# Twenty short VectorE memsets and fifty-one one-element ScalarE copies at the start of a channel-attention kernel

## The chip, the cores and the metric

The kernel runs on one core of one Trainium2 chip. The metric is the device time of one execution in microseconds (us). Before the change it was 743.04 us, the median of 3 runs (742.54 to 744.04).

## The reference, cut to what matters

```python
H = W = 384; C = 384; r = C // 4          # x is (1, H, W, C) bf16, w1 (C, r), w2 (r, C)

def reference(x, w1, w2):
    xf = x.reshape(B, H * W, C)
    gap = jnp.mean(xf, 1)                 # mean over all pixels, per channel
    gmp = jnp.amax(xf, 1)                 # maximum over all pixels, per channel
    h_a = relu(gap @ w1)                  # (written as h * (h > 0))
    h_m = relu(gmp @ w1)
    scale = sigmoid(h_a @ w2 + h_m @ w2)
    return x * scale[:, None, None, :]
```

The scale needs all of `x` before any of the output can be written. So the kernel has a reading half (sums and maxima), a short turn in which the scale is made, and a storing half (multiply and store; what did not fit on chip is read again). On chip, `x` lies in six buffers, the slots.

## The kernel before

All engines share the tile `small`; the first lines fill its constants. ScalarE's only early work is a one-element Sigmoid.

```python
small = consts.tile([P, 16], BF16)
ones_bf = small[:, 0:1]
hid = small[0:R, 8:9]
hid_a = small[0:R, 10:12].bitcast(F32)
nc.vector.memset(ones_bf, 1.0)
pick = small[0:NQP, 10:10 + 2 * CQ].bitcast(F32)
nc.vector.memset(pick, 0.0)
for q in range(CQ):
    nc.vector.memset(pick[q * QP:q * QP + 1, q:q + 1], 1.0)
...
nc.scalar.activation(out=scale_bc[0:1, 0:1], in_=pick[0:1, 0:1], func=ACT.Sigmoid)
acc = consts.tile([P, A, C], BF16)
slots = [xpool.tile([P, n, C], BF16, name=f"x{s}") for s, n in enumerate(SLOTS)]
...
# reading half, one round per load: SyncE loads, TensorE sums, VectorE keeps the maximum
nc.sync.dma_start(out=rows[:, a:b, :], in_=...)
sums(rows, m, done, TOT - tail_rows)
nc.vector.tensor_tensor(out=acc[:, 0:k, :], in0=acc[:, 0:k, :], in1=rows[:, j:j + k, :], op=ALU.max)
...
# the turn, ScalarE's branch (mean) and VectorE's branch (maximum), which meet in hid
nc.scalar.activation(out=hid_a, in_=hTa_ps, func=ACT.Relu)
...   # acc folded to one row, transposed on TensorE, reduced, multiplied with w1
nc.vector.scalar_tensor_tensor(out=hid, in0=hTm_ps, scalar=0.0, in1=hid_a, op0=ALU.max, op1=ALU.add)
nc.tensor.matmul(z_ps, lhsT=hid.to_broadcast([R, P]), rhs=w2_sb, start=True, stop=True)
nc.scalar.activation(out=scale_bc, in_=z_ps, func=ACT.Sigmoid)
...
# storing half: VectorE multiplies, ScalarE issues the store, SyncE reads the next block into the slot
```

Of the kernel before, what the change touches and what calls it, by code (L numbers as in the profile page):

```python
# [32 lines left out]
ACC_STORES_AT = 3  # L33
SUM_TAIL = 2
MM_ROWS = 4


@with_exitstack
def kernel(
# [7 lines left out]
    nc = tc.nc  # L47
# [36 lines left out]
    small = consts.tile([P, 16], BF16)  # L84
# [8 lines left out]
    nc.vector.memset(pick, 0.0)  # L93
    for q in range(CQ):
        nc.vector.memset(pick[q * QP:q * QP + 1, q:q + 1], 1.0)
    ident_bf = consts.tile([P, P], BF16)
    make_identity(nc, ident_bf)

# [5 lines left out]
        scale_bc[0:NQP, 0:2 * P].bitcast(F32),  # L104
    ]
    nc.scalar.activation(out=scale_bc[0:1, 0:1], in_=pick[0:1, 0:1], func=ACT.Sigmoid)
    acc = consts.tile([P, A, C], BF16)
    slots = [xpool.tile([P, n, C], BF16, name=f"x{s}") for s, n in enumerate(SLOTS)]

# [3 lines left out]
    kept_ps = psum.tile([P, PSUM_ROWS, C], BF16)  # L113
    sum_ps = bank_a[0:NQP, 0:MM_ROWS * P]
    nc.vector.memset(bank_a, 0.0)
# [23 lines left out]
    def sums(rows, n, done, total):  # L139
        for k in range(0, n, MM_ROWS):  # L140
            g = min(MM_ROWS, n - k)
            for q in range(CQ):
                nc.tensor.matmul(  # L143
                    sum_ps[q * QP:q * QP + 1, 0:g * P],
                    lhsT=ones_bf[:, 0:1],
                    rhs=rows[:, k:k + g, q * P:(q + 1) * P],
                    start=(done + k == 0),
                    stop=(done + k + g == total),
                )

    def turn_sums():

        for r in range(MM_ROWS):
            nc.scalar.copy(out=s_sb[r % 2], in_=sum_ps[:, r * P:(r + 1) * P])
# [163 lines left out]
```

## Time and profile before

| | before |
|---|---|
| time, median of 3 | 743.04 us |
| bytes moved, mean rate | 312.32 MB, 421 GB/s |
| busy: VectorE (DVE), TensorE (PE), ScalarE (ACT) | 66%, 17%, 0% |
| DMA share in the turn, 268 to 277 us | 0.43 |

From the page of the kernel before: busy us of each engine with its share of the span and number of instructions; then the busy tenths of the 16 DMA engines and their GB/s in 40 equal slices; then the DMA queues with packets, MB and share of the engines' time.

```profile
PE 127.2 (17%) x966; PEld 40.6 (5%) x966; DVE 489.4 (66%) x168; ACT 3.3 (0%) x9; POOL 0.7 (0%) x6
DMA  9999999999999969999999999999999999999997
GB/s 383 423 435 434 433 430 418 428 429 426 427 422 422 418 254 378 402 435 446 432 431 428 432 437 436 436 432 432 427 434 437 436 436 432 432 427 432 441 437 340
q1 hardware_dynamic: 12032, 198.92, 63.2%
q8 instruction: 7, 0.11, 0.1%
q14 instruction: 4, 0.03, 0.0%
```

The DMA row is at nine tenths everywhere but in the turn and at the end: the kernel is bound by its transfers. ScalarE does next to nothing. The two "instruction" queues carry the engines' own instructions, 16 KB a packet on q8 and 8 KB on q14 (0.11 MB over 7, 0.03 MB over 4).

The timeline of the kernel before, VectorE and then ScalarE from the start. Columns: start, duration, engine, line, operation, output and input with their shapes, count, and in brackets how long the engine was idle and what ended that.

```profile
0.81 0.06 DVE L89 MEMSET small<- 128x1 bf16 x1 [0.81 <-PEq L302]
1.48 0.27 DVE L95 MEMSET small<- 1x1 f32 x3
7.18 1.26 DVE L179 COPY acc<-x_79 128x4224 bf16<-128x4224 bf16 x1 [5.44 <-DMA x_79<-in_x_dram]
0.73 1.28 ACT L106 ACT_TABLE_LOAD   x1 [0.73 <-PEq L302]
2.03 0.20 ACT L106 ACTIVATE scale_bc<-small 1x1 bf16<-1x1 f32 x1
266.97 0.26 ACT L154 COPY w_sb<-bank_a 65x128 f32<-65x128 f32 x1 [264.74 <-PE bank_a L143]
```

VectorE has nothing to do from 1.75 to 7.18 us, because the first tile is still on its way. ScalarE has nothing from 2.23 to 266.97 us. These two holes are where the change puts its instructions.

The view by windows of the kernel before: length, busy us (and instructions) of PE, PEld, DVE, ACT and POOL, granted clock, DMA share, GB/s.

```profile
268.00:277.00 9.00, 4.28 (x64) 3.47 (x63) 6.84 (x10) 1.27 (x5) 0.00 (x0) 0.50 0.43 115
```

And the end of the turn in the chain of work that ended last (start, duration, what):

```profile
275.61 0.17 DVE small L219
275.82 0.51 PE bank_a L220
276.41 0.50 ACT scale_bc L221
```

In the turn the DMA engines wait for the scale, so lateness there should go into the time in full.

### The profile page before, as it was taken

How to read it: one execution, taken by the hardware profiler on the slowest of the kernel's cores; microseconds unless marked ns; L12 is line 12 of the kernel's file. 1: busy time of each engine (PE TensorE's matmuls, PEld its weight loads, DVE VectorE, ACT ScalarE, POOL GpSimd, SP SyncE). 2: the span in 40 equal slices, each digit the busy share in tenths (PEclk: the TensorE clock that was granted, in tenths of full speed). 3: DMA queues.
4: the chain of work that ended last, by engine and by line, in shares of the span. 5: the costliest groups of instructions: out<-in, count | busy, mean ns of one | idle time of the engine just before them, and what ended most of it. 6: DMA issues, size and time to landing. Idle time of an engine off the chain costs nothing.

```text
span 741.5 us, 2477 instructions
## 1 busy us (share of the span) xinstructions
PE 127.2 (17%) x966; PEld 40.6 (5%) x966; DVE 489.4 (66%) x168; ACT 3.3 (0%) x9; POOL 0.7 (0%) x6
## 2 busy tenths in 40 slices
PE   3345443445454550000000000000000000000000
PEld 0011111111111120000000000000000000000000
DVE  6789999999999989999444443444444444444600
ACT  0000000000000000000000000000000000000000
POOL 0000000000000000000000000000000000000000
PEclk9865666655555555555555555555555555555555
DMA  9999999999999969999999999999999999999997
GB/s 383 423 435 434 433 430 418 428 429 426 427 422 422 418 254 378 402 435 446 432 431 428 432 437 436 436 432 432 427 434 437 436 436 432 432 427 432 441 437 340
DMA packets 18379, 312.32 MB, mean 421 GB/s; under 512 B 2400, under 2 KB 3008, under 8 KB 6592
## 3 DMA queue, kind: packets, MB, share of 16 engines
q1 hardware_dynamic: 12032, 198.92, 63.2%
q10 hardware_dynamic: 6336, 113.25, 35.7%
q8 instruction: 7, 0.11, 0.1%
q14 instruction: 4, 0.03, 0.0%
HBM read 198.92 MB, written 113.25 MB: 421 GB/s over the span
## 4 chain that ended last, share of the span: by engine, by line
another core or an unknown queue 44%; DMA 34%; DVE 14%; DVEq 1%; SPq 1%; issue 1%; PE 0%; ACT 0%; ACTq 0%
DMA x_81<-in_x_dram 9%; DMA x_82<-in_x_dram 7%; DVE acc L183 7%; DMA out_dram<-x_83 6%; DMA x_79<-in_x_dram 6%; DMA x_80<-in_x_dram 3%; DMA x_83<-in_x_dram 3%; DVE x_81 L226 1%; DVE x_80 L226 1%; DVE x_83 L226 1%; DVE x_82 L226 1%; DVE x_79 L226 1%; DVEq L313 1%; SPq L253 1%
## 5 line engine op out<-in xcount | busy, mean ns | idle before, releaser
L226 DVE TENSOR_TENSOR x_79<-x_79,scale_bc 128x16896 bf16<-128x16896 bf16 (+6 forms) x13 | 45.4, 3538 | 34.2 <-DMA x_79<-in_x_dram 33.0
L226 DVE TENSOR_TENSOR x_80<-x_80,scale_bc 128x16896 bf16<-128x16896 bf16 (+4 forms) x9 | 40.9, 4576 | 28.7 <-DMA x_80<-in_x_dram 28.7
L226 DVE TENSOR_TENSOR x_84<-x_84,scale_bc 128x16896 bf16<-128x16896 bf16 x4 | 35.8, 8958 | 33.1 <-DMA x_84<-in_x_dram 33.1
L226 DVE TENSOR_TENSOR x_83<-x_83,scale_bc 128x16896 bf16<-128x16896 bf16 x4 | 35.8, 8956 | 33.0 <-DMA x_83<-in_x_dram 33.0
L226 DVE TENSOR_TENSOR x_82<-x_82,scale_bc 128x16896 bf16<-128x16896 bf16 x4 | 35.8, 8957 | 32.8 <-DMA x_82<-in_x_dram 32.8
L226 DVE TENSOR_TENSOR x_81<-x_81,scale_bc 128x16896 bf16<-128x16896 bf16 (+3 forms) x6 | 36.0, 6021 | 31.0 <-DMA x_81<-in_x_dram 31.0
L183 DVE TENSOR_TENSOR acc<-acc,x_84 128x4224 bf16<-128x4224 bf16 (+3 forms) x21 | 47.3, 2253 | 5.4 <-DMA x_84<-in_x_dram 4.7
L143 PEld LDWEIGHTS <-small 128*1 128x1 bf16 x900 | 36.4, 110 | 229.9 <-issue 227.0
L183 DVE TENSOR_TENSOR acc<-acc,x_83 128x4224 bf16<-128x4224 bf16 (+1 forms) x19 | 42.8, 2253 | 1.3 <-DMA x_83<-in_x_dram 0.7
L183 DVE TENSOR_TENSOR acc<-acc,x_80 128x4224 bf16<-128x4224 bf16 (+1 forms) x18 | 40.6, 2257 | 3.0 <-DMA x_80<-in_x_dram 2.4
L183 DVE TENSOR_TENSOR acc<-acc,x_79 128x4224 bf16<-128x4224 bf16 (+1 forms) x17 | 38.9, 2287 | 1.5 <-DMA x_79<-in_x_dram 1.0
L183 DVE TENSOR_TENSOR acc<-acc,x_81 128x4224 bf16<-128x4224 bf16 (+2 forms) x17 | 37.9, 2229 | 1.5 <-DMA x_81<-in_x_dram 1.0
L183 DVE TENSOR_TENSOR acc<-acc,x_82 128x4224 bf16<-128x4224 bf16 x16 | 37.7, 2358 | 1.5 <-DMA x_82<-in_x_dram 1.0
L143 PE MATMUL bank_a<-x_84,small 128*1 128x512 bf16 (+2 forms) x165 | 21.6, 558 | 27.1 <-DMA x_84<-in_x_dram 27.1
L143 PE MATMUL bank_a<-x_79,small 128*1 128x512 bf16 (+1 forms) x150 | 20.4, 574 | 28.7 <-DMA x_79<-in_x_dram 28.7
L143 PE MATMUL bank_a<-x_80,small 128*1 128x512 bf16 (+3 forms) x150 | 21.0, 585 | 23.6 <-DMA x_80<-in_x_dram 23.6
L143 PE MATMUL bank_a<-x_83,small 128*1 128x512 bf16 (+2 forms) x159 | 20.3, 540 | 23.3 <-DMA x_83<-in_x_dram 23.3
L143 PE MATMUL bank_a<-x_82,small 128*1 128x512 bf16 (+2 forms) x138 | 19.6, 594 | 20.9 <-DMA x_82<-in_x_dram 20.9
L143 PE MATMUL bank_a<-x_81,small 128*1 128x512 bf16 (+3 forms) x138 | 19.4, 593 | 21.1 <-DMA x_81<-in_x_dram 21.1
L179 DVE COPY acc<-x_79 128x4224 bf16<-128x4224 bf16 x1 | 1.3, 1260 | 5.4 <-DMA x_79<-in_x_dram 5.4
L185 DVE COPY kept_ps<-x_79 128x3072 uint32<-128x3072 uint32 x1 | 3.4, 3354 | 0.0
L226 DVE TENSOR_TENSOR x_81<-kept_ps,scale_bc 128x6144 bf16<-128x6144 bf16 x1 | 3.4, 3350 | 0.0
(39 smaller groups left out, 22.5 us busy)
## 6 DMA issues: line engine op xcount, KB each, us to landing
x_84<-in_x_dram SPq DMA_DIRECT2D x5, 4224.0 KB, 27.4
x_79<-in_x_dram SPq DMA_DIRECT2D x5, 4224.0 KB, 27.4
x_80<-in_x_dram SPq DMA_DIRECT2D x5, 4224.0 KB, 27.7
x_81<-in_x_dram SPq DMA_DIRECT2D x5, 4224.0 KB, 27.4
x_82<-in_x_dram SPq DMA_DIRECT2D x5, 4224.0 KB, 27.4
x_83<-in_x_dram SPq DMA_DIRECT2D x4, 4224.0 KB, 27.4
out_dram<-x_82 ACTq DMA_DIRECT2D x4, 4224.0 KB, 74.3
out_dram<-x_83 ACTq DMA_DIRECT2D x4, 4224.0 KB, 71.1
```

The source lines that it names most:

```text
L143: nc.tensor.matmul(sum_ps[q * QP:q * QP + 1, 0:g * P], lhsT=ones_bf[:, 0:1], rhs=rows[:, k:k + g, q * P:(q + 1) * P], start=(done + k == 0 ...
L179: nc.vector.tensor_copy(out=acc, in_=rows[:, 0:A, :])
L183: nc.vector.tensor_tensor(out=acc[:, 0:k, :], in0=acc[:, 0:k, :], in1=rows[:, j:j + k, :], op=ALU.max)
L185: nc.vector.tensor_copy(out=kept_ps.bitcast(U32), in_=rows.bitcast(U32))
L226: nc.vector.tensor_tensor(out=dst, in0=src, in1=scale_bc.unsqueeze(1).to_broadcast([P, n, C]), op=ALU.mult)
L253: nc.sync.dma_start(out=slots[s][:, j:j + m, :], in_=rows_of(xr, first, n)[:, j:j + m, :])
L313: with _tile.TileContext(nc) as tc:
```

## The change

It adds 20 memsets of one element on VectorE and 51 copies of one element on ScalarE, near the start. They write columns of `small` that nothing reads. Their only possible use is to delay these two engines a little or to shift what comes later in their instruction streams.

```diff
+FILLS = (20, 51)
 ...
     for q in range(CQ):
         nc.vector.memset(pick[q * QP:q * QP + 1, q:q + 1], 1.0)
+    for _ in range(FILLS[0]):
+        nc.vector.memset(small[0:1, 9:10], 0.0)
 ...
     nc.scalar.activation(out=scale_bc[0:1, 0:1], in_=pick[0:1, 0:1], func=ACT.Sigmoid)
+    for _ in range(FILLS[1]):
+        nc.scalar.copy(out=small[0:1, 1:2], in_=small[0:1, 0:1])
```

## The prediction

> **What bounds the kernel now.** The page gives 312.32 MB moved in a span of 741.5 us at a mean of 421 GB/s; its DMA row shows 9 tenths in every slice but two. DVE is busy 66%, PE 17%, ACT 0% (3.3 us). The kernel is bound by DMA transfers; at the 432 GB/s that most slices show, 312.32 MB alone would take about 723 us (an estimate from the page). The other 18 us are the start (0 to 5 us: DMA share 0.67 in the view by windows), the turn between the reading half and the storing half (268 to 277 us: 0.43, 115 GB/s) and the last stores, draining after 703 us.
>
> **What the change adds.** It removes and moves nothing. By the timeline, one-element memsets on VectorE take 59 ns and start about 0.105 us apart (1.48, 1.59, 1.69 us). Twenty more are 2.1 us, so VectorE's opening work ends near 3.9 us in place of 1.75 us. A one-element ACTIVATE took 204 ns; two consecutive copies of line 154 started 0.16 us apart. Fifty-one copies are then an estimated 8 to 13 us, from 2.2 us to 10 to 15 us. ACT's busy time should go from 3.3 to 9 to 14 us.
>
> **How much is on the critical path.** None that I can find. VectorE waits 5.4 us for the first tile and starts its first real work at 7.18 us. ScalarE does nothing between 2.23 and 266.97 us, and issues its first store at 277.3 us. The first loads are issued by SyncE, between 0.74 and 3.2 us, waiting for no engine. The fills write bytes of `small` that nobody else uses. The first LDWEIGHTS at 4.39 us waits for a VectorE memset; should it wait for the last fill, that is near 3.9 us, before the data that it needs anyway. Should it wait for ScalarE's copies too, the first sums come some 8 us late, but two queued loads keep the DMA busy to 25 us and PE is a third busy, so this is caught up.
>
> **Fills also shift the instruction streams.** The Trainium skill ("Runtime: NRT & Kernel Launch", Instruction fetch mechanics) says an engine's instructions are refilled in 16 KiB blocks by a DMA queue of its own, mostly hidden. The trace agrees in part: 16,384-byte instruction packets on q8, but 8,192-byte ones on q14, at 111.2, 224.3, 280.7 and 376.8 us, each taking 0.3 to 0.6 us on one DMA engine. By instruction counts I take the first and third for VectorE's and the last for ScalarE's. With the fills, VectorE's should move to about 70 and 266 us and ScalarE's to about 276 us, into the turn, perhaps with one more for ScalarE later. No engine stalls at these fetches in the trace (VectorE runs back to back over 280.7 us). I put their worth at under 0.5 us either way.
>
> **Prediction:** 743.0 us, 8 in 10 between 741.2 and 744.8. Faster by over 2%: 0.01; within 2%: 0.97; slower by over 2%: 0.02.
>
> **Right if:** 20 memsets before 7 us and 51 copies before 15 us in the timeline; the first VectorE copy still near 7.2 us and SyncE's loads at the same times; the turn and the 20 us per block in the storing half unchanged; bytes and GB/s the same. **Wrong if:** a later first load, PE starting after 10 us with a gap in DMA, or other times in the turn.
>
> **What would make it wrong:** a sequencer's stall at a moved instruction fetch, just where the scale is finished and the first stores are issued; a tile-wide dependence that ties VectorE or loads to the copies; a reordering of other instructions.

## The result, and the profile after

The time after is 743.33 us (median of 6 runs, 742.4 to 744.74), against 742.91 us before (6 runs, 742.04 to 744.04). The ratio is 1.0005, with a 95% interval of 0.9994 to 1.0016: the same. A ratio here is the mean time of one kernel's runs over that of the other's of the same rounds, so it is not quite the ratio of the medians quoted.

The page after, in the lines that answer to those of before:

```profile
PE 131.8 (18%) x966; PEld 41.3 (6%) x966; DVE 490.6 (66%) x188; ACT 14.3 (2%) x61; POOL 0.7 (0%) x6
DMA  9999999999999969999999999999999999999998
q1 hardware_dynamic: 12032, 198.92, 63.1%
q8 instruction: 7, 0.11, 0.1%
q14 instruction: 4, 0.03, 0.0%
```

ACT's busy time rose by 11.0 us and the DMA row is as it was. The number of instruction packets did not change either. The timeline after, VectorE, then ScalarE, then TensorE's first weight load (the kernel's lines have moved down by 2 to 6):

```profile
0.85 0.06 DVE L99 MEMSET small<- 1x1 bf16 x1
1.50 0.27 DVE L97 MEMSET small<- 1x1 f32 x3
1.82 2.14 DVE L99 MEMSET small<- 1x1 bf16 x19
7.24 1.26 DVE L185 COPY acc<-x 128x4224 bf16<-128x4224 bf16 x1 [3.28 <-DMA x<-in_x_dram]
0.73 1.28 ACT L112 ACT_TABLE_LOAD   x1 [0.73 <-PEq L308]
2.02 0.19 ACT L112 COPY small<-small 1x1 bf16<-1x1 bf16 x1
2.23 1.28 ACT L110 ACT_TABLE_LOAD   x1
3.53 0.20 ACT L110 ACTIVATE scale_bc<-small 1x1 bf16<-1x1 f32 x1
3.64 11.19 ACT L112 COPY small<-small 1x1 bf16<-1x1 bf16 x50
267.04 0.26 ACT L160 COPY w_sb<-bank_a 65x128 f32<-65x128 f32 x1 [252.22 <-PE bank_a L149]
4.39 0.12 PEld L149 LDWEIGHTS <-small 128*1 128x1 bf16 x4 [4.39 <-DVE small L99]
```

The idle time in brackets tells the story. VectorE's wait for the first tile fell from 5.44 to 3.28 us and ScalarE's for the sums from 264.74 to 252.22 us; the work after each wait starts where it did (7.18 and 7.24 us, 266.97 and 267.04 us). One thing is new: one copy was scheduled ahead of the Sigmoid, so ScalarE loads its table twice, 1.28 us each, in the same hole. And the first weight load, which reads `small`, is now put down to a fill memset (L99); the fills end at 3.96 us and it starts at 4.39 us, as before.

The turn after, in the view by windows, is that of before to 0.01 of DMA share:

```profile
268.00:277.00 9.00, 4.35 (x64) 3.54 (x64) 6.85 (x10) 1.34 (x5) 0.00 (x0) 0.50 0.43 114
```

The packet records of the trace give the start of each 8,192-byte instruction packet on q14:

```
before   111.2   224.3   280.7   376.8 us
after     70.8   224.2   269.5   271.2 us
```

Three of the four moved, two of them into the turn. The time did not follow.

### The profile page after: what moved, and what is told of

Same layout as the page of the kernel before. It is cut to its first block, busy times and chain, and to the rows that moved or that the text cites. A ratio compares the mean times of both kernels' runs of the same rounds, so it can differ in the third digit from the quotient of the medians.

```text
span 741.6 us, 2549 instructions
## 1 busy us (share of the span) xinstructions
PE 131.8 (18%) x966; PEld 41.3 (6%) x966; DVE 490.6 (66%) x188; ACT 14.3 (2%) x61; POOL 0.7 (0%) x6
## 4 chain that ended last, share of the span: by engine, by line
another core or an unknown queue 40%; DVE 28%; DMA 24%; DVEq 1%; issue 1%; SPq 1%; PE 0%
DVE acc L189 22%; DMA x<-in_x_dram 17%; DMA out_dram<-x 6%; DVE x L232 5%; DVEq L319 1%; SPq L259 1%; DMA acc<-in_x_dram 1%; DVE kept_ps L191 0%; DVE acc L209 0%; DVE acc L232 0%; DVE acc L185 0%; SPq L176 0%; DVE bank_b L193 0%; PE bank_a L219 0%
## 5 line engine op out<-in xcount | busy, mean ns | idle before, releaser
L232 DVE TENSOR_TENSOR x<-x,scale_bc 128x16896 bf16<-128x16896 bf16 (+11 forms) x40 | 229.1, 5768 | 194.9 <-DMA x<-in_x_dram 193.8
L189 DVE TENSOR_TENSOR acc<-acc,x 128x4224 bf16<-128x4224 bf16 (+4 forms) x108 | 245.3, 2271 | 14.1 <-DMA x<-in_x_dram 10.7
L149 PE MATMUL bank_a<-x,small 128*1 128x512 bf16 (+2 forms) x900 | 126.8, 590 | 140.2 <-DMA x<-in_x_dram 140.1
L112 ACT COPY small<-small 1x1 bf16<-1x1 bf16 x51 | 9.8, 193 | 1.6
L185 DVE COPY acc<-x 128x4224 bf16<-128x4224 bf16 x1 | 1.3, 1259 | 3.3 <-DMA x<-in_x_dram 3.3
L191 DVE COPY kept_ps<-x 128x3072 uint32<-128x3072 uint32 x1 | 3.4, 3352 | 0.0
L232 DVE TENSOR_TENSOR x<-kept_ps,scale_bc 128x6144 bf16<-128x6144 bf16 x1 | 3.4, 3350 | 0.0
L209 DVE TENSOR_TENSOR acc<-acc 128x384 bf16<-128x384 bf16 (+2 forms) x4 | 2.6, 659 | 0.1
L232 DVE TENSOR_TENSOR acc<-acc,scale_bc 128x1920 bf16<-128x1920 bf16 (+1 forms) x2 | 2.5, 1253 | 0.2 <-DMA acc<-in_x_dram 0.2
L99 DVE MEMSET small<- 1x1 bf16 x20 | 1.2, 59 | 1.1
L166 PEld LDWEIGHTS <-x 128*128 128x128 bf16 x48 | 1.5, 108 | 0.0
L112 ACT ACT_TABLE_LOAD x1 | 1.3, 1283 | 0.7 <-PEq L308 0.7
L110 ACT ACT_TABLE_LOAD x1 | 1.3, 1283 | 0.0
```

Source lines behind the costliest of these rows:

```text
L112: nc.scalar.copy(out=small[0:1, 1:2], in_=small[0:1, 0:1])
L149: nc.tensor.matmul(sum_ps[q * QP:q * QP + 1, 0:g * P], lhsT=ones_bf[:, 0:1], rhs=rows[:, k:k + g, q * P:(q + 1) * P], start=(done + k == 0 ...
L166: nc.tensor.matmul(gsum_ps[:, q:q + 1], lhsT=rows[:, k, q * P:(q + 1) * P], rhs=ones_bf, start=False, stop=(last and k == n - 1 and q == C ...
L185: nc.vector.tensor_copy(out=acc, in_=rows[:, 0:A, :])
L191: nc.vector.tensor_copy(out=kept_ps.bitcast(U32), in_=rows.bitcast(U32))
L209: nc.vector.tensor_tensor(out=acc[:, 0:h, :], in0=acc[:, 0:h, :], in1=acc[:, n - h:n, :], op=ALU.max)
```

## The experiments

The theory is slack: the fills sit in idle time, and only what goes beyond that idle time costs. Rivals: the two halves of the change cost and gain and cancel; short fills on a nearly idle engine are free wherever they stand; the instruction fetches (the DMA transfers that bring an engine its next instructions) that more instructions need have a cost of their own. Experiments of one call ran on the same chip and share the runs of the kernel before.

### Each half alone

```diff
-FILLS = (20, 51)
+FILLS = (20, 0)     # v20_only
+FILLS = (0, 51)     # a51_only
```

> Only the 20 VectorE memsets. Slack theory (the fills sit in idle time before the first tile): ratio to the kernel before 1.000, within 0.2%; first VectorE copy within 0.1 us of 7.2 us. Rival, cancelling (each half costs or gains some us and the two halves offset): this half alone differs by 0.3% or more, about 2 us, from the kernel before. Instruction-fetch theory: VectorE's fetches move to about 71 and 270 us, ScalarE's stays at 377 us, no time with it.

> Only the 51 ScalarE copies. Slack theory: ratio 1.000 within 0.2%; the copies end near 15 us, 250 us before ScalarE's next work. Cancelling rival: differs by 0.3% or more, opposite in sign to the other half. Fetch theory: ScalarE's fetch at about 271 us in place of 377 us, VectorE's at 111 and 281 us as before.

Measured: 743.07 us with the memsets alone (ratio 1.0003, interval 0.999 to 1.0017) and 742.99 us with the copies alone (1.0001, 0.9988 to 1.0015), against 742.9 us. Neither half does anything that can be seen, so no cancelling of effects of some tenths of a per cent is at work. The q14 packets also tell whose they are:

```
v20_only    71.1   224.4   270.9   376.5 us
a51_only   110.9   224.5   269.4   280.6 us
```

The memsets move the packets of 111 and 281 us to 71 and 271 us, so those are VectorE's. The copies move that of 377 us to 269 us, so it is ScalarE's. That of 224 us stays in both.

### The same number of instructions in another place

Fifty-one copies in place on `hid_a` in the turn, and in a second kernel 20 copies of 1x3 elements in place on `acc`, between the last maximum and the transposes. Each is pinned, since the next step reads what it writes. The results stay correct. In the second one the operation is a copy and not a memset, because it must not change `acc`.

```diff
 # turn_a51
     nc.scalar.activation(out=hid_a, in_=hTa_ps, func=ACT.Relu)
+    [nc.scalar.copy(out=hid_a[0:1, 0:1], in_=hid_a[0:1, 0:1]) for _ in range(51)]
 # turn_v20, after the last folding step of acc
+    [nc.vector.tensor_copy(out=acc[0:1, 0, ::P], in_=acc[0:1, 0, ::P]) for _ in range(20)]
```

> The same number of one-element ScalarE copies, but in the turn: in place on hid_a, after its Relu, so that the sum into hid must wait for them. Slack theory: the place decides; 51 x 0.224 us = 11.4 us from 271.5 us end at about 282.9 us, where hid was made at 275.67 us, so all later work comes about 7.2 us late and the time is about 7.2 us, 1.0%, longer. Rival (short fills on ScalarE are free wherever they stand, since ScalarE is 0% busy): ratio 1.000.

> Twenty tiny VectorE copies (1x3, in place on acc) between the last maximum and the transposes. Slack theory: nothing covers them there; 20 x 0.105 to 0.15 us = 2.1 to 3 us later scale, and 2.1 to 3 us (0.3 to 0.4%) longer time. Rival (free wherever they stand): ratio 1.000.

Measured: turn_a51 749.29 us, ratio 1.009 (1.0076 to 1.0104), about 6.7 us longer; turn_v20 746.77 us, ratio 1.0053 (1.0039 to 1.0066), about 3.9 us longer. The timeline of turn_a51, ScalarE and VectorE:

```profile
271.44 11.28 ACT L195 COPY small<-small 1x1 f32<-1x1 f32 x51
282.75 0.16 DVE L219 SCALAR_TENSOR_TENSOR small<-bank_a,small 96x1 bf16<-96x1 f32 x1 [7.45 <-ACT small L195]
```

Fifty-one copies took 11.28 us here and 11.4 us at the start; VectorE now waits 7.45 us for them before it can make `hid` (at 275.61 us before, 282.75 us here). About 4 us of the 11.28 us are still hidden, behind the maximum's branch. "ScalarE is 2% busy" does not make its instructions free. VectorE in the timeline of the kernel before, then in that of turn_v20:

```profile
274.73 0.43 DVE L214 TENSOR_REDUCE small<-bank_a 128x2 bf16<-128x256 bf16 x1 [0.56 <-PE bank_b L213]
```

```profile
275.11 3.84 DVE L204 COPY acc<-acc 1x3 bf16<-1x3 bf16 x20
279.51 0.43 DVE L214 TENSOR_REDUCE small<-bank_a 128x2 bf16<-128x256 bf16 x1 [0.56 <-PE bank_b L213]
```

The twenty copies took 3.84 us, 0.19 us each, where I had expected 0.105 to 0.15 us by the memsets. The wait after them (0.56 us) is that of before, so all of it is exposed, and the time grew by it. The Trainium skill ("VectorE: DVE Perf Modes", The TRN2 errata) says that operations with a source in SBUF pay a fixed extra latency for each instruction, which weighs most on small ones. The traces fit that, but do not single it out: a one-element memset, which has no source, took 59 ns, a 1x3 copy 159 ns, and the two also differ in operation, in size, and in that each copy reads what the one before it wrote.

### How large VectorE's hole is

The memsets were tied to `acc`, so that they precede the first maximum; no ScalarE copies.

```diff
-    acc = consts.tile([P, A, C], BF16)
+    acc = consts.tile([P, A, C], BF16)
+    [nc.vector.memset(acc[0:1, 0, 0:1], 0.0) for _ in range(120)]    # v120; 250 in v250
```

In v250 SyncE's instructions were held in program order, since the scheduler would otherwise have moved the loads of two free slots forward (no run on record shows that); the order of loads is that of before in v120 and v250 alike. In both, the scheduler put two copies of rows of `x` to PSUM, where TensorE's sums lie (L185, L187; in the kernel before they follow the first copy to `acc`), in among the memsets.

> 120 VectorE memsets pinned before the first maximum (they write acc, which the first copy overwrites), no ScalarE copies. They are about 13 us, 3.5 to 5.4 us of them in the idle time before the first tile. VectorE is then some 8 us late, but two queued loads keep the DMA busy to 25 us and VectorE has 4.2 us idle at 25 us and about 9.6 us in the rest of the reading half. Slack theory: within 1 us of the kernel before (0 to 0.15%). Rival (the early chain of waits is VectorE's, so its lateness is paid in full): about 8 us, 1.1% longer.

> 250 VectorE memsets pinned so, loads in their old order. About 28 us; VectorE is some 24 us late, the two queued loads are in by 25.5 us, the next can be issued only at about 38 us: 11 to 15 us (1.5 to 2%) longer by the slack theory. Rival of full payment: 22 to 24 us (3.1%) longer. Rival that early VectorE work is free: 1.000.

Measured: v120 744.83 us, ratio 1.0021 (1.0005 to 1.0037), about 1.6 us longer; v250 758.13 us, ratio 1.0198 (1.0183 to 1.0213), about 14.7 us longer; before 743.26 us. VectorE in the timeline of v120, from the last of the memsets:

```profile
11.94 9.85 DVE L107 MEMSET acc<- 1x1 bf16 x82
21.82 1.26 DVE L179 COPY acc<-x 128x4224 bf16<-128x4224 bf16 x1
```

In v120 SyncE could issue the reload of the second slot at 27.3 us in place of 16.2 us, 11 us late, and nearly all of that was absorbed. The 1.6 us are a little over what I expected. In the profiled run the second load had already landed 1.0 us late (8.1 for 7.1 us), before VectorE could matter; but in turn_v20 such a lateness (0.9 us) was gone by the seventh load. The trace shows two other parts. The queued loads did just run out: from 20 to 30 us the DMA share is 0.92 in place of 1.01, an estimated 0.9 us of transfer time. And load 15 landed 1.28 us late but load 16 1.96 us (134.14 for 132.18 us), just after a q14 packet of 132.07 us, by the counts VectorE's: a step like those of a1000 below. How the 1.6 us divide was not tested. In v250 the view by windows shows what ran out, first before, then v250:

```profile
27.00:40.00 13.00, 6.67 (x57) 2.09 (x52) 12.37 (x6) 0.00 (x0) 0.00 (x0) 0.74 1.04 448
```

```profile
27.00:40.00 13.00, 3.64 (x30) 1.11 (x25) 8.64 (x79) 0.00 (x0) 0.00 (x0) 0.75 0.13 39
```

The queued loads were in and no slot was free: the DMA share fell from 1.04 to 0.13 over 13 us, some 12 us of transfer time (and from 0.95 to 0.85 over the 27 us before that, nearly 3 us more). So VectorE has two reserves: the 5.4 us wait for the first tile, and then the loads that are already queued. Only when both are used up does the kernel pay, and then with DMA time.

### How large ScalarE's hole is, and what 1000 copies cost inside it

```diff
-FILLS = (20, 51)
+FILLS = (20, 1000)     # a1000
+FILLS = (20, 1300)     # a1300
```

> 20 memsets and 1000 ScalarE copies at the beginning. Slack theory: 3.6 + 999 x 0.224 us end at about 227 us, before ScalarE's next work at 267 us, so ratio 1.000 within 0.2%. Fetch rival (an instruction fetch costs some tenths of a us to the kernel): some 7 or 8 more 8 KB fetches on q14, so 2 to 8 us (0.3 to 1%) longer.

> 1300 ScalarE copies, past the end of its idle time. Slack theory: they end at about 294.6 us, so the first copy of the sums comes 27.5 us late; some 4 us of that are covered, since ScalarE's path through the turn waits 5 us for the maximum's, so the time is about 23.5 us (3.2%) longer. Rival (ScalarE is off the critical path, whatever it does): ratio 1.000.

Measured: a1300 769.59 us, ratio 1.0358 (1.0339 to 1.0376), about 26.6 us longer. Its timeline, ScalarE and VectorE:

```profile
3.64 291.85 ACT L112 COPY small<-small 1x1 bf16<-1x1 bf16 x1299
295.39 0.25 ACT L160 COPY w_sb<-bank_a 65x128 f32<-65x128 f32 x1
300.94 0.16 DVE L225 SCALAR_TENSOR_TENSOR small<-bank_a,small 96x1 bf16<-96x1 f32 x1 [0.26 <-PE bank_a L224]
```

ScalarE's first copy of the sums came 28.4 us later than before (295.39 less 266.97 us) and `hid` 25.3 us later (300.94 less 275.61 us): past the hole the copies are paid for, less about 3 us of cover in the turn (4 expected). The remaining 1.3 us of the 26.6 us were not followed up.

The surprise is a1000: 746.9 us, ratio 1.0047 (1.003 to 1.0064), about 3.5 us longer, though its copies end inside the hole. ScalarE in its timeline, then its instruction queue on the page:

```profile
3.64 224.45 ACT L112 COPY small<-small 1x1 bf16<-1x1 bf16 x999
270.64 0.26 ACT L160 COPY w_sb<-bank_a 65x128 f32<-65x128 f32 x1 [42.55 <-PE bank_a L149]
```

```profile
q14 instruction: 12, 0.10, 0.0%
```

ScalarE waited 42.55 us for the sums and was on no one's path. Yet the sums came at 270.64 us in place of 266.97 us: the reading half itself took 3.7 us longer. There were 8 more instruction packets. This is what the fetch rival had said (2 to 8 us), and against the slack theory as I had stated it. VectorE was not slowed: its 98 maxima of 128x4224 elements took 2358.2 ns on average in both traces. The loads were late. When SyncE's nth load had landed, in us:

```
load         before   after   wide450    a700    a1000
13            107.1   107.1     107.0   107.6    108.0
16            132.2   132.2     132.2   133.4    133.8
22            162.5   162.5     162.6   164.4    164.8
27            187.8   187.7     187.8   189.7    190.8
33            218.2   218.1     218.2   220.0    221.8
45            251.5   251.4     252.1   253.3    255.2
```

The lateness of a1000, 0.3 us up to load 12, then grows in steps of 0.6 to 0.7 us, at loads 13, 16, 22, 27 and 33. Its q14 packets that are ScalarE's start at 17.2, 45.4, 73.6, 103.1, 131.4, 159.9, 189.0 and 217.5 us; each of the last five falls just before one of these steps. The packet records do not name the DMA engine, but let one follow it: in these records, while transfers are queued, a packet starts within some 4 ns of the end of another. This, followed so, is the engine that took the fetch of 103.1 us (start, end, queue, bytes):

```
100.632  101.886   q1   33792
101.882  103.136   q1   33792
103.133  103.442   q14   8192
103.439  105.070   q1   33792
```

The fetch takes 0.31 us and the load packet after it 1.631 us in place of 1.254 us: together this engine falls 0.69 us behind the other fifteen. This engine ends its part of load 13 at 107.58 us, the next slowest at 106.68 us, and the load counts as landed only at 108.0 us: it waits for its last engine. Why this engine was the last already is taken up below.

### Is it the fetches, or a busy ScalarE?

Two kernels separate them. wide450 keeps ScalarE busy as long with fewer instructions; a700 has an intermediate number of fetches.

```diff
-FILLS = (20, 51)
+FILLS = (20, 450)      # wide450; (20, 700) in a700, with the copy line unchanged
 ...
-        nc.scalar.copy(out=small[0:1, 1:2], in_=small[0:1, 0:1])
+        nc.scalar.copy(out=scale_bc[0:1, :], in_=small[0:1, 0:1].to_broadcast([1, C]))
```

> 450 ScalarE copies of 384 elements in place of 1000 of one: about 0.5 us each, so ScalarE is busy about as long as with the 1000 (to some 200 to 235 us), with only 3 or 4 instruction fetches of its own in the reading half in place of 8. Fetch theory (each fetch holds up one DMA engine by about 0.7 us, always the same one, and only what goes beyond the lag of other engines shows): 0 to 0.9 us, ratio 1.000 to 1.001. Rival (a busy ScalarE slows the reading half by itself): as with 1000 copies, 3.5 us, 1.0047.

> 700 one-element ScalarE copies, done by about 161 us. Fetch theory: fetches near 17, 45, 74, 103, 131 and 160 us; by the loads of the run with 1000 copies the reading half is then 2.3 us late and stays so, ratio 1.003. Slack theory alone: 1.000.

Measured: wide450 743.55 us against 743.48 us, ratio 1.0002 (0.9989 to 1.0014); a700 744.95 us, ratio 1.0021 (1.0007 to 1.0034), about 1.5 us longer, somewhat under the 0.3% expected. The timeline and the instruction queue of wide450, then of a700:

```profile
2.26 243.43 ACT L112 COPY scale_bc<-small 1x384 bf16<-1x384 bf16 x450
267.58 0.26 ACT L160 COPY w_sb<-bank_a 65x128 f32<-65x128 f32 x1 [21.89 <-PE bank_a L149]
```

```profile
q14 instruction: 8, 0.06, 0.0%
```

```profile
3.64 156.99 ACT L112 COPY small<-small 1x1 bf16<-1x1 bf16 x699
q14 instruction: 9, 0.07, 0.0%
```

In wide450 ScalarE's copies went on for longer than in a1000 (243.43 us against 224.45 us) and its copies wrote 384 times as much each, but the time is that of before. So it is not ScalarE's work, but its number of instructions. The table of loads above agrees: wide450 is on time up to load 33 and 0.6 us late at the end; a700 steps with its fetches at 102.7, 131.6 and 160.1 us, is 1.9 us late at load 22 and then stays so: its copies end at 160.6 us.

Why do the first fetches cost little? This part is read from one profiled run of each kernel and was not tested by itself. The 16 KB packets on q8, seven in every run whatever was added to VectorE and ScalarE, I take for TensorE's, which has the most instructions in the kernel before (1932 of 2477). The same following of engines shows that they hold up a DMA engine too. In the trace of before, the engine that took the one of 39.9 us (1.06 us long) ended its part of the next load at 46.46 us, when the next slowest ended at 44.97 us: 1.5 us of lag. TensorE's packets of 39.9, 82.4 and 121.4 us were on three different engines. ScalarE's four packets from 45.4 to 131.4 us in a1000 were all on one, and so were the five of a700 from 45.0 to 160.1 us. (Later packets cannot be followed as surely, since the engines' times come to overlap.) So TensorE's fetches do not add up in one place, and ScalarE's do: by this account the first two hide behind the lag of 1.5 us that another engine has already, the third in part, and each further one shows at once. In a1000 this engine ends its part of a load at 56.10 us, still before TensorE's at 56.55 us; two fetches later it is the last, by the 0.9 us given above.

## Why the prediction was right

The prediction was 743.0 us, between 741.2 and 744.8 us, and 743.33 us was measured. Point by point:

- **VectorE's fills lie in the wait for the first tile.** Right. 20 x 0.105 us was 2.1 us; the trace has 2.14 us for nineteen, and the wait shrank from 5.44 to 3.28 us. v250 shows where this ends.
- **ScalarE's fills lie in its hole of 264 us.** Right. They end at 14.83 us (8 to 13 us from 2.2 us predicted, so 10 to 15 us). Of ACT's 14.3 us, slightly over the 9 to 14 us predicted, 1.3 us are the second table load.
- **The first weight load might wait for the last memset, and it would not matter.** Right: the profile names a fill as what it waited for, and it starts at 4.39 us as before.
- **No reordering, no change of the turn.** Right where it matters. One copy was put before the Sigmoid and one memset before the clearing of a PSUM bank; both are off the path.
- **VectorE's fetches to about 70 and 266 us, ScalarE's to about 276 us.** Right in kind: 70.8 us, and 269.5 and 271.2 us. The attribution by counting was confirmed by the two halves alone. The further ScalarE fetch that it thought possible did not come.
- **Fetches are worth under 0.5 us either way.** Right for this change, but it had not seen why. The change moves three fetches and adds none, and no load of the table above lands later for it: load 33 at 218.1 us for 218.2 us. A fetch is not worth under 0.5 us in general. It can hold an engine up by 0.69 us, and eight more cost 3.5 us. So this point was in part luck: nothing in the prediction looked at where a moved fetch falls, and in v120 a single one of VectorE's, at 132.07 us, came just before a step of 0.7 us.

A change of over 2% either way had been given a chance of 0.03; the interval found reaches 0.16%. What the prediction lacked was the second way in which fills can cost: it weighed a stall of the sequencer at a fetch, which no trace shows here, and not the DMA engine's lag, which a1000 shows.

## What to carry to other kernels

Cost an added instruction at the place where it stands, by the idle time in brackets just before the engine's next real work and by what is already queued behind that: the same 51 copies cost nothing in a hole of 264 us and 6.7 us in the turn. A change in the number of instructions has a second cost in a kernel bound by DMA, because instruction fetches use the same DMA engines as the data. It is hidden up to the lag that some engine has anyway, so test it with ten or twenty times the dose before calling it zero.

## What the Trainium skill lacked or had wrong

- "Runtime: NRT & Kernel Launch", Instruction fetch mechanics: it gives blocks of 16 KiB for all engines and calls the crossing of a block mostly hidden. Here TensorE's packets had 16,384 bytes, but those of VectorE and ScalarE 8,192 bytes. Crossings were hidden in the kernel and the change, but not in a1000, where 8 more made the kernel 3.5 us (0.47%) longer.
- No page says on which DMA engine an engine's instruction fetches run. Here four of ScalarE's in a row were on one and held it up by 0.69 us each (0.31 us for the packet, 0.38 us for the slower one after it), while TensorE's first three were on three.
- "DMA: Bandwidth & Descriptors", Queues, rings and completion order, says that each engine takes turns among its queues, a whole packet (typically about 9 to 17 descriptors) at a time. Here the fetch of 103.133 us went in after the fifth of the eight transfers of 33,792 bytes that the engine had of one load; the trace calls each of these a packet, and whether they are packets in the page's sense is not shown. The page gives no figure for what such a turn costs the load: here 0.69 us of delay on that engine.
- "ScalarE: Activation LUTs", What ACT_TABLE_LOAD costs: it gives about 1283 ns and a drain of about 1380 ns for every switch. Here the load took 1.28 us, and the next instruction started 0.01 us (2.02 us) and 0.02 us (3.53 us) after it; no such drain shows, nor before the second load, which began 0.02 us after the copy ahead of it (2.23 us).
